# Values of the later batches in halves of 32 queries by 64 keys, a tile of their own for the gates' fifth part, and another order of layer two's mixes

## The chip, the cores and the metric

The kernel runs on one core of one Trainium2 chip. The metric is the device time in microseconds of one execution, the median of three runs. The engines of the core are TensorE (PE; its weight loads are listed as PEld), VectorE (DVE), ScalarE (ACT), GpSimd (POOL), and SyncE (SP), which issues most transfers.

## The reference

Three steps stand one behind the other. `q`, `k` and `v` have 4 batches, 8 heads, 576 positions and 64 columns a head; the two layers have 512 columns outside and 2048 inside, for 4 x 576 = 2304 tokens.

```python
scores = scale * np.matmul(q, k.transpose(0, 1, 3, 2))
mask_plain = (rel >= 0) & (rel < 32)                          # heads 0 to 3
mask_dil = (rel >= 0) & (rel < 32 * 4) & (rel % 4 == 0)       # heads 4 to 7
attn = softmax(np.where(mask, scores, -1e9))
x = np.matmul(attn, v)             # heads side by side: 2304 x 512
h = x @ w_in1;  g = h - np.tanh(h);             x = g @ w_out1
h = x @ w_in2;  g = h * (1 / (1 + np.exp(-h))); out = g @ w_out2
```

A query sees 32 keys: its own and the 31 before it, in the dilated heads every fourth. With the positions of the dilated heads sorted by their remainder by 4, both kinds are a band of 32.

## The kernel before

**Attention.** The work goes by pairs: a pair is two heads (j = 0, 1) of one batch, 16 pairs in all, four for each batch. The 576 queries of a pair are cut into NB = 9 blocks of QB = 64; a block needs the KB = 96 keys from 32 before its first query to its last. The first batch (`first`) is worked in units of three blocks, with masks added in TensorE and the probabilities transposed by TensorE. From the second batch on, `transpose` turns q and k on VectorE, `products` makes scores in four tiles of TensorE at a time (two heads on separate rows, two groups of 32 queries on separate columns, each against its own 64 keys), `masks` adds the mask `near` on VectorE, and `maxima`, `exps` (ACT), `norm` follow. `p_quarter` transposes the probabilities, 32 by 32, into `pT`, which has keys on its partitions: four calls for each head, with the two corners that no query sees left at zero. `values` then makes, for each block and head, one matmul: `v` (96 keys by 64 columns) is stationary, `pT` (96 keys by 64 queries) moves, and the two heads go to separate columns of the array. The outputs are evicted twice: `x_hi` copies to the rounded part of X on ACT, `x_lo` takes the rest on VectorE. `GROUPS` splits the blocks of a pair into 5 and 4, one PSUM bank each (tiles `s` and `o`). X is a ring of two batches; columns whose place is still in use go to `late` first.

**Order.** Everything up to the first block of tokens of layer one, with the first two batches of attention, is put in order by `play`, a list scheduler that knows a cost in us for each step on each engine (`op({"T": 1.45}, ...)`) and takes what can begin first, then by rank. The later batches are put by hand into numbered ticks between the matmuls of layer one (`plan`): at a pair's tick `score`, the values of the pair before it (`other`) come first, into a bank of `ps_h` (blocks 0 to 7) and the free end of bank `o` (block 8), then the scores; then the next v is loaded.

**Layer one** goes by blocks of 512 tokens: 16 times 12 matmuls for h and 12 for y (three for each product, since weights and activations are split into a leading and a trailing part). Meanwhile the weights of layer two are prepared and stored.

**Layer two** works on 768 tokens at a time (three `Group`s) and makes each 2 by 2 product with seven instead of eight. `mixes` makes the sums and differences of x that it needs, as steps: `whole` adds the two parts of a quarter of x, `minus` takes a difference, `lead` copies the rounded part (ACT), `trail` takes the rest (VectorE). A group has eight quads (`quad`): `products`, `sums`, `gates`, which fill `G[:, quad, 0:4]`. The second product of the first group has sixteen steps f; in step f the split of the gates for step f + 2 (`parted`: ACT's copy to `gs`, VectorE's difference) comes first, then what `IN_TWO` has for f, then a load of the next group's x (f = 3 to 6) or two steps of its `mixes` (f = 7 on). In the quads of the first group `IN_ONE` puts steps that prepare `w_out2`: `out_bits`, `out_plain`, `out_mixed`. The raw words of half of these lie in `G[..., 4, :]`, the fifth part of the gates' tile, which the first group does not need; the later groups keep a sum of gates there (`combine`).

Of the kernel before, what the change touches and what calls it, by code (L numbers as in the profile page):

```python
# [35 lines left out]
def tile_kernel(  # L36
# [198 lines left out]
    GROUPS = ((0, (NB + 1) // 2), ((NB + 1) // 2, NB))  # L235

    NM = NB + GROUPS[0][1]
# [18 lines left out]
    near = cpool.tile([P, NM, NARROW], BF16, name="near")  # L256
    pT = cpool.tile([KB, NB, 2, QB], F32, name="pT")
    nc.gpsimd.memset(pT, 0.0)

    class Pair:  # L260
# [49 lines left out]
        def v_tile(self):  # L310
            if self.first and not self.dil:
                self.v = [opool.tile([KB, NB, D], F32, tag="wout", name="v") for _ in range(2)]
            else:
                if self.first and self.c == NPAIR - 1:
                    vt = g_tile([KB, 2, NB, D], F32, "v")
                else:
                    vt = inpool.tile([KB, 2, NB, D], F32, tag="v", name="v")
# [5 lines left out]
        def v_loads(self):  # L323
# [15 lines left out]
            for j in range(2):  # L339
                src = v[b, h0 + j]  # L340
                s0 = src[QB - HALO:]
                out.append(lambda e, j=j, src=src: e.dma_start(out=self.v[j][HALO:, 0, :], in_=src[0:QB]))
                out.append(lambda e, j=j, s0=s0: e.dma_start(
                    out=self.v[j][:, 1:, :],
                    in_=bass.AP(s0.tensor, s0.offset, [[D, KB], [QB * D, NB - 1], [1, D]])))
            return out

# [158 lines left out]
        def values(self, n0, n1, bank):  # L506
# [7 lines left out]
            if self.dil:  # L514
                parts = [(a, b, src[:, a - s0:b - s0]) for a, b in self.cut(s0, s1)]
            else:
                i0, i1 = s0 // DIL, s1 // DIL
                src = src.rearrange("p (i r) -> p i r", r=DIL)

                m = DIL - (self.b > 0)  # L520
                last = CLS * (DIL - 1)
                parts = [] if m == DIL else [(a, b, src[:, a - last - i0:b - last - i0, DIL - 1]) for a, b in self.cut(last + i0, last + i1)]
            out = [(self.columns(a, b), x) for a, b, x in parts]
            if not self.dil:
                a = self.column(0)
# [1067 lines left out]
```

## Time and profile before

| | |
|---|---|
| three runs | 844.59, 847.73, 846.69 us; median 846.69 |
| profiled execution | 845.14 us, its span from the first to the last instruction 843.4 us |
| TensorE busy | 828.2 us, 98% of the span, 6103 matmul records |
| VectorE, ACT, POOL busy | 68%, 50%, 24% |
| granted TensorE clock | 1.00 |
| moved by DMA | 184.58 MB, 219 GB/s in the mean |

One execution of the program is profiled. Times are us from the span's start unless marked ns. Matmuls are pipelined, so a busy TensorE is not TensorE at its peak, and the durations of records overlap; an fp32 matmul leaves two records. L408 is the line of the scores of the later batches, L510 that of the values, L578 that of all matmuls of the two layers, L748 and L749 the two steps of `parted`, L679 to L689 the steps of `mixes` (`whole`, `minus`, `lead`, `trail`).

### The profile page before, as it was taken

The page shows a single profiled execution, that of the slowest core. Times are in us where ns is not written, and L with a number is a line of the kernel's source. Part 1 is how long each engine was busy: PE and PEld are TensorE (multiplying, and loading weights), DVE is VectorE, ACT ScalarE, POOL GpSimd, SP SyncE. Part 2 cuts the span into 40 slices and gives each one's busy share as a digit, 9 for nine tenths or more (in the row PEclk, how much of TensorE's full clock was granted, in tenths as well). Part 3 has the DMA queues.
Part 4 walks back from the last instruction along what each step waited for, and adds up shares of the span by engine and source line. Part 5 has one row for each costly group of instructions (what it writes and reads, how often), then busy time and mean ns, then how long its engine had stood idle before and what let it go on. Part 6 is the DMA issues. An engine that isn't in the chain of part 4 may idle for free.

```text
span 843.4 us, 16397 instructions
## 1 busy us (share of the span) xinstructions
PE 828.2 (98%) x6103; PEld 734.7 (87%) x6103; DVE 570.5 (68%) x1010; ACT 423.6 (50%) x960; POOL 199.5 (24%) x236
## 2 busy tenths in 40 slices
PE   8899999999999999999999999999999999999998
PEld 5777778888887888888899999887999999999997
DVE  4688987466676664566665677548767888567764
ACT  5898976355555442666543343445322554233442
POOL 8555542143333331111100000001025100054000
PEclk9999999999999999999999999999999999999999
DMA  9997253655569424577679299659898677898542
GB/s 221 298 238 182 73 138 91 179 125 122 126 163 235 99 60 138 180 256 263 263 262 349 75 363 366 232 161 373 266 408 275 238 292 265 328 351 288 187 169 57
DMA packets 169856, 184.58 MB, mean 219 GB/s; under 512 B 88849, under 2 KB 132913, under 8 KB 168753
## 3 DMA queue, kind: packets, MB, share of 16 engines
q1 hardware_dynamic: 168944, 182.69, 66.9%
q8 instruction: 48, 0.79, 0.4%
q0 software_dynamic: 832, 0.85, 0.4%
q14 instruction: 32, 0.25, 0.1%
HBM read 137.89 MB, written 45.61 MB: 218 GB/s over the span
## 4 chain that ended last, share of the span: by engine, by line
PE 75%; DVE 4%; ACT 3%; DMA 1%; SPq 1%; issue 1%; POOL 1%; DVEq 0%; ACTq 0%; POOLq 0%
PE y L578 37%; PE h L578 22%; PE q L578 14%; DMA w_out<-o_mixed 1%; ACT prob L469 1%; DVE m L1215 1%; SPq L301 1%; PE h L510 1%; DVE pT L492 1%; PE s L408 0%; DVE tmp L717 0%; DVE g L605 0%; ACT gg L1451 0%; DMA o_raw<-in_moe_w_out_dram 0%; PE o L408 0%
## 5 line engine op out<-in xcount | busy, mean ns | idle before, releaser
L578 PE MATMUL y<-gg,w 128*128 128x512 f32 (+1 forms) x960 | 218.3, 370 | 2.7 <-DVE gg L1148 2.6
L578 PE MATMUL h<-x,w 128*128 128x512 f32 (+1 forms) x960 | 218.3, 370 | 0.7 <-POOL w L203 0.7
L578 PEld LDWEIGHTS y<-gg,w 128*128 128x128 f32 x960 | 167.2, 189 | 34.7 <-DVE gg L1148 3.9
L578 PEld LDWEIGHTS h<-x,w 128*128 128x128 f32 x960 | 167.3, 189 | 31.7 <-POOL w L203 1.1
L578 PE MATMUL y<-wr,gs 128*128 128x256 f32 (+1 forms) x840 | 123.5, 298 | 0.0
L578 PEld LDWEIGHTS y<-wr,gs 128*128 128x128 f32 x840 | 112.6, 191 | 4.6
L749 DVE TENSOR_TENSOR gs<-G,gs 128x768 fp32r<-128x768 f32 x72 | 70.3, 982 | 43.6 <-ACT gs L748 43.2
L748 ACT ACTIVATE gs<-G 128x768 fp32r<-128x768 f32 x72 | 60.0, 843 | 73.4 <-PE y L578 41.8
L726 ACT ACTIVATE G<-tmp 128x384 f32<-128x384 f32 (+1 forms) x48 | 33.0, 686 | 116.3 <-DVE tmp L717 116.3
L578 PE MATMUL q<-x,wr 128*128 128x384 f32 x432 | 82.7, 334 | 0.2 <-DVE tmp L717 0.2
L605 DVE TENSOR_TENSOR g<-h,g 128x512 f32<-128x512 f32 (+1 forms) x64 | 39.8, 621 | 58.8 <-ACT g L604 58.5
L763 POOL TENSOR_TENSOR G<-G 128x768 f32<-128x768 f32 (+1 forms) x24 | 42.3, 1777 | 152.1 <-DVE G L727 151.5
L578 PEld LDWEIGHTS q<-x,wr 128*128 128x128 f32 x432 | 75.5, 188 | 0.5 <-DVE tmp L717 0.5
L1451 ACT ACTIVATE gg<-g 128x512 fp32r<-128x512 f32 (+1 forms) x64 | 37.0, 579 | 75.1 <-DVE g L605 74.0
L1453 DVE TENSOR_TENSOR gg<-g,gg 128x512 fp32r<-128x512 f32 (+1 forms) x64 | 40.4, 631 | 41.7 <-ACT gg L1451 38.9
L604 ACT ACTIVATE g<-h 128x512 f32<-128x512 f32 (+1 forms) x64 | 34.6, 541 | 67.5 <-PE h L578 65.0
L727 DVE SCALAR_TENSOR_TENSOR G<-G,tmp 128x384 f32<-128x384 f32 (+1 forms) x48 | 41.4, 862 | 34.4 <-ACT G L726 34.4
L578 PE MATMUL h<-x,wr 128*128 128x384 f32 x288 | 57.8, 335 | 1.0 <-ACT tmp L721 1.0
L578 PE MATMUL y<-x,wr 128*128 128x384 f32 x288 | 57.8, 335 | 0.0
L194 POOL TENSOR_TENSOR st<-st 128x512 int32<-128x512 int32 x36 | 39.6, 1109 | 76.5 <-DVE st L190 41.7
L578 PE MATMUL q<-wr,gs 128*128 128x256 f32 (+1 forms) x348 | 57.6, 301 | 0.0
L578 PEld LDWEIGHTS h<-x,wr 128*128 128x128 f32 x288 | 50.4, 188 | 1.4 <-ACT tmp L721 1.3
(163 smaller groups left out, 1136.4 us busy)
## 6 DMA issues: line engine op xcount, KB each, us to landing
wr<-w_in SPq DMA_DIRECT2D x72, 512.0 KB
wr<-w_out SPq DMA_DIRECT2D x66, 512.0 KB
st<-in_moe_w_in_dram SPq DMA_DIRECT2D x32, 256.0 KB
st<-in_moe_w_out_dram SPq DMA_DIRECT2D x16, 512.0 KB
st_in<-in_moe_w_in_dram SPq DMA_DIRECT2D x32, 256.0 KB
w_in<-mixed SPq DMA_DIRECT2D x8, 1024.0 KB
wr<-w_in SPq DMA_DIRECT2D x24, 256.0 KB
x<-y_hi SPq DMA_DIRECT2D x6, 768.0 KB
```

The lines of the kernel that those rows point to most:

```text
L194: engine.tensor_tensor(out=high, in0=high, in1=self.low.bitcast(I32), op=ALU.add)
L301: nc.sync.dma_start(out=t[p0:p0 + 32].rearrange("r (n d) -> r n d", d=32), in_=src[b, h0 + j, :, 32 * e:32 * e + 32].rearrange("(n r) d -> ...
L578: nc.tensor.matmul(o, stat[a], mov[b], start=first and n == 0, stop=last and n == 2, skip_group_check=more)
L604: nc.scalar.activation(out=g, in_=h, func=AF.Tanh)
L605: nc.vector.tensor_tensor(out=g, in0=h, in1=g, op=ALU.subtract)
L726: nc.scalar.activation(out=g, in_=h, func=AF.Tanh, scale=0.5)
L727: return lambda: nc.vector.scalar_tensor_tensor(out=g, in0=g, scalar=1.0, in1=h, op0=ALU.add, op1=ALU.mult)
L748: nc.scalar.activation(out=gs[:, 0], in_=g, func=AF.Copy)
L749: nc.vector.tensor_tensor(out=gs[:, 1], in0=g, in1=gs[:, 0].bitcast(F32), op=ALU.subtract)
L763: (on or nc.vector).tensor_tensor(out=out, in0=x, in1=y, op=op)
L1451: nc.scalar.activation(out=gg[:, 0], in_=g, func=AF.Copy)
L1453: nc.vector.tensor_tensor(out=gg[:, 1], in0=g, in1=gg[:, 0].bitcast(F32), op=ALU.subtract)
```

## The change

From the second batch on each block's values are made in two halves: queries 0 to 31 against keys 0 to 63, and queries 32 to 63 against keys 32 to 95. The first half lies on partitions 0 to 63, the second on 64 to 127, so that v needs its rows 32 to 63 once more on partitions 96 to 127; a transfer inside SBUF puts them there, two ticks after the loads (in the second batch behind them). Each half has a bank of its own. The groups become 6 and 3 blocks, for room in bank `o`. The zeroing of `pT` goes, the mask has 13 instead of 14 blocks, and `near` is made in five copies that wait for the first pair's first unit. In layer two the fifth part of G becomes a tile `E` (before that, raw words under the same tag), `out_mixed(4)` is cut into its differences (quad 3) and its splits (quad 4), and the mixes come in another order. The cost of the second batch's values in the scheduler goes from 1.45 to 0.95, those of their evictions to 0.7 each.

```diff
-    GROUPS = ((0, (NB + 1) // 2), ((NB + 1) // 2, NB))
-    NM = NB + GROUPS[0][1]
+    GROUPS = ((0, 2 * UB), (2 * UB, NB))
+    NM = NB + 1 + UB
+    NEAR_M = NB + GROUPS[0][1]
...
-    near = cpool.tile([P, NM, NARROW], BF16, name="near")
-    pT = cpool.tile([KB, NB, 2, QB], F32, name="pT")
-    nc.gpsimd.memset(pT, 0.0)
+    near = cpool.tile([P, NEAR_M, NARROW], BF16, name="near")
+    pT1 = cpool.tile([P, NB, 2, QB], F32, name="pT")
+    pT = pT1[:KB]
+    pT2 = pT1.rearrange("p n j q -> p (n j q)")[:, :NB * QB].rearrange("p (n j q) -> p n j q", n=NB, j=2)
...
+        def double_v(self):
+            nc.sync.dma_start(out=self.vt[KB:], in_=self.vt[32:64])
...
-                other.values(0, NB - 1, ps_h.tile([P, 512], F32, tag="h", name="h"))
-                other.values(NB - 1, NB, banks[1][:, (NB - GROUPS[1][0]) * NARROW:])
+                other.halves([ps_h.tile([P, 512], F32, tag="h", name="h"), banks[1][:, (NB - GROUPS[1][0]) * NARROW:]])
...
-                for n0 in (0, NB - 1):
-                    other.x_hi(nc.scalar, n0)
-                    other.x_lo(n0)
+                for i in range(2):
+                    other.x_hi(nc.scalar, i)
+                    other.x_lo(i)
...
-            i, kk = n // 2, n // 2 + n % 2
+            i, kk = divmod(n, 2)
             p0 = QB * j + 32 * i
-            nc.vector.transpose(
-                out=pT[32 * kk:32 * kk + 32, :, j, 32 * i:32 * i + 32],
-                in_=self.p[p0:p0 + 32, :, 32 * (kk - i):32 * (kk - i) + 32],
-            )
+            k0 = KB - 32 * kk if i else 32 * kk
+            nc.vector.transpose(out=pT2[k0:k0 + 32, :, j], in_=self.p[p0:p0 + 32, :, 32 * kk:32 * kk + 32])
...
+        def halves(self, banks):
+            o = [bank[:, :NB * 32].rearrange("p (n q) -> p n q", q=32) for bank in banks]
+            for n in range(NB):
+                for i in range(2):
+                    for j in range(2):
+                        r = slice(64 * i, 64 * i + 64)
+                        nc.tensor.matmul(o[i][64 * j:64 * j + 64, n], self.v[j][r, n], pT2[r, n, j], start=True, stop=True)
...
-            return [whole(p, 4), whole(r, 3), minus(u, r, p), lead(7, u), whole(w, 1), minus(p, p, w), lead(5, p),
-                    trail(7, u), minus(r, r, p), lead(6, r), trail(5, p), whole(u, 2), minus(u, u, r), lead(4, u),
-                    trail(6, r), trail(4, u)]
+            return [whole(p, 4), whole(r, 3), minus(u, r, p), whole(w, 1), lead(7, u), minus(p, p, w), trail(7, u),
+                    lead(5, p), minus(r, r, p), trail(5, p), lead(6, r), whole(u, 2), minus(u, u, r), trail(6, r),
+                    lead(4, u), trail(4, u)]
...
-            a, b, c, d, e = (G[:, q:q + count, k] for k in range(5))
+            a, b, c, d = (G[:, q:q + count, k] for k in range(4))
+            e = E[:, q:q + count]
...
+    DOUBLE = 2
...
+        at(s0 + score + DOUBLE, p.double_v)
...
-        narrows = [op({"V": 0.35, "P": 0.9}, lambda e, g=g: narrow(e, g), [], NEXT0 - 12, port=True) for g in range(4)]
+        narrows = [op({"V": 0.35, "P": 0.9}, lambda e, g=g: narrow(e, g), x_done[0][:1], NEXT0 - 30, port=True) for g in range(4)]
+        narrows.append(op({"V": 0.15, "P": 0.3}, more, narrows, NEXT0 - 30, port=True))
...
-            return [op({"S": 0.55}, fn, [hold], r - 5 + 0.01 * n, 0.4) for n, fn in enumerate(p.v_loads())]
+            loads = [op({"S": 0.55}, fn, [hold], r - 5 + 0.01 * n, 0.4) for n, fn in enumerate(p.v_loads())]
+            return loads if p.b > 1 else [*loads, op({"S": 0.55}, lambda e, p=p: p.double_v(), loads, r - 4, 0.8)]
...
-            a = op({"T": 1.45}, lambda e, p=p: p.all_values(), [*ts, *v_in, *left["bank"]], r + 14)
+            a = op({"T": 0.95}, lambda e, p=p: p.all_values(), [*ts, *v_in, *left["bank"]], r + 14)
...
-                raw = G.bitcast(U32)[:, 4 * e:4 * e + 4, 4, :2 * P].rearrange("p k (n two) -> p k n two", two=2)
+                if e == 0:
+                    pairs_raw[q] = gates.tile([P, 2, 4, P, 2], U32, tag="E", name="raw")
+                raw = pairs_raw[q][:, e]
...
-                  3: [lambda: out_mixed(4), lambda: out_loads(6)]}
+                  3: [lambda: out_sums(4), lambda: out_loads(6)], 4: [lambda: out_split(4)]}
...
-                    G = gates.tile([P, NF // 2, 5, HALF], F32, name="G")
+                    G = gates.tile([P, NF // 2, 4, HALF], F32, name="G")
...
+                E = gates.tile([P, NF // 2, HALF], F32, tag="E", name="E")
```

In `halves`, behind the matmuls, the two banks' evictions are set up as in `values`, cut at the same columns of X and `late`, with runs of 32 queries (plain heads: 8 by 4) instead of whole blocks.

## Rows read from the trace of the kernel before

**Rows 1.** The page's busy time, share and instructions of the engines.

```profile
PE 828.2 (98%) x6103; PEld 734.7 (87%) x6103; DVE 570.5 (68%) x1010; ACT 423.6 (50%) x960; POOL 199.5 (24%) x236
```

**Rows 2.** Waits of TensorE over the span: total us, times, longest.

```profile
PE y L578 <- DVE gg L1148: 2.6, 3, 1.7
...
PE h L578 <- ACT tmp L721: 1.0, 1, 1.0
...
PE y L578 <- ACT gs L748: 0.4, 1, 0.4
```

**Rows 3.** Timeline of TensorE, 181 to 186.5: start, us, what, count.

```profile
182.25 1.15 PE L510 MATMUL h<-pT,v 96*64 96x64 f32 x32
183.23 0.29 PE L510 MATMUL o<-pT,v 96*64 96x64 f32 x4
183.45 0.76 PE L408 MATMUL s<-kT,qT 64*32 64x64 f32 x40
...
184.59 2.11 PE L578 MATMUL h<-x,w 128*128 128x512 f32 x8
```

**Rows 4.** Lines L510 and L408: ns min/median/max, first and last start.

```profile
L510 PEld LDWEIGHTS h<-pT,v x224: 132/138/139, 182.2 to 306.0; 96*64 96x64 f32 x112
L510 PE MATMUL h<-pT,v x224: 221/222/270, 182.2 to 306.1; 96*64 96x64 f32 x112
...
L408 PEld LDWEIGHTS s<-kT,qT x480: 102/107/108, 47.4 to 306.9; 64*32 64x32 f32 x160
```

**Rows 5.** Groups by form, whole span: busy us, mean ns, idle before.

```profile
L372 PE MATMUL h<-late,qin 96*64 96x96 f32 x48 | 2.9, 255 | 1.0 <-ACT kT L146 1.0
```

**Rows 6.** Timeline of SP's queue, 199 to 218.

```profile
202.44 7.46 SPq L335 DMA_DIRECT2D v<-in_v_dram  x13
```

**Rows 7.** Timeline of VectorE, 0 to 24.

```profile
7.97 0.96 DVE L148 COPY near<-mask 32x896 bf16<-32x896 bf16 x2 [6.52 <-POOL mask L224]
```

**Rows 8.** The chain that ended last, in order of time, around the fourth quad.

```profile
490.78 2.08 PE q L578 x12
...
514.33 2.08 PE q L578 x12
521.61 2.08 PE q L578 x12
```

**Rows 9.** Timeline of all engines, 494 to 516.

```profile
507.70 1.30 ACT L1376 ACTIVATE m<-m 128x512 fp32r<-128x512 f32 x2 [1.82 <-DVE m L1215]
507.92 0.41 DVE L1215 TENSOR_TENSOR m<-raw,m 128x256 f32<-128x256 f32 x1
...
508.91 0.47 ACT L721 ACTIVATE tmp<-h 128x384 f32<-128x384 f32 x1
...
509.43 1.32 PE L578 MATMUL h<-x,wr 128*128 128x384 f32 x6 [0.97 <-ACT tmp L721]
```

**Rows 10.** The same chain, in the second product of the first group.

```profile
565.77 1.36 PE q L578 x6
...
569.85 1.36 PE q L578 x6
...
587.50 1.38 PE q L578 x6
```

**Rows 11.** Timeline of all engines, 570 to 590.

```profile
576.55 0.95 DVE L683 TENSOR_TENSOR tmp<-tmp 128x768 f32<-128x768 f32 x1
...
579.15 0.96 DVE L749 TENSOR_TENSOR gs<-G,gs 128x768 fp32r<-128x768 f32 x1 [1.65 <-ACT gs L748]
579.21 2.92 PE L578 MATMUL y<-room,gs 128*128 128x512 f32 x12
...
581.83 0.94 DVE L679 TENSOR_TENSOR tmp<-x 128x768 f32<-128x768 f32 x1
...
583.71 0.84 ACT L748 ACTIVATE gs<-G 128x768 fp32r<-128x768 f32 x1 [2.31 <-POOL G L194]
```

**Rows 12.** Timeline of SP's queue, 579.5 to 581.

```profile
580.10 0.33 SPq L1199 DMA_DIRECT2D wr<-w_in  x1
```

More of the change, by code (lines that the diff above doesn't have):

```diff
@@ L316, in v_tile @@
                 else:
-                    vt = inpool.tile([KB, 2, NB, D], F32, tag="v", name="v")
+                    vt = inpool.tile([KB if self.first else P, 2, NB, D], F32, tag="v", name="v")
                 self.vt = vt
@@ L514, in values @@
             if self.dil:
-                parts = [(a, b, src[:, a - s0:b - s0]) for a, b in self.cut(s0, s1)]
+                out = [([X[:, w, self.c, self.column(s0):self.column(s0) + s1 - s0] for w in range(2)], src)]
             else:
[L517 to L522, printed above, removed]
@@ L523, in values @@
-            out = [(self.columns(a, b), x) for a, b, x in parts]
-            if not self.dil:
                 a = self.column(0)
-                x = X[:, :, self.c, a:a + CLS * m].rearrange("p w (r i) -> p w i r", i=CLS)[:, :, i0:i1]
-                out.append(([x[:, w] for w in range(2)], src[:, :, :m]))
+                x = X[:, :, self.c, a:a + S].rearrange("p w (r i) -> p w i r", i=CLS)[:, :, s0 // DIL:s1 // DIL]
+                out = [([x[:, w] for w in range(2)], src.rearrange("p (i r) -> p i r", r=DIL))]
@@ L528, in values @@
             self.left[n0] = out
+        def halves(self, banks):
[5 more added lines that the diff above has]
+                        nc.tensor.matmul(o[i][64 * j:64 * j + 64, n], self.v[j][r, n], pT2[r, n, j], start=True, stop=True)
+            for i in range(2):
+                if self.dil:
+                    out = [([d.rearrange("p (n i q) -> p n i q", i=2, q=32)[:, :, i] for d in self.columns(a, b)],
+                            o[i][:, a // QB:b // QB]) for a, b in self.cut(0, S)]
+                else:
+                    e = 32 // DIL
+                    src = o[i].rearrange("p n (e r) -> p n e r", r=DIL)
+                    last, a, m = CLS * (DIL - 1), self.column(0), DIL - 1
+                    x = X[:, :, self.c, a:a + CLS * m].rearrange("p w (r n i e) -> p w n i e r", r=m, i=2, e=e)[:, :, :, i]
+                    out = [([d.rearrange("p (n i e) -> p n i e", i=2, e=e)[:, :, i] for d in self.columns(a, b)],
+                            src[:, (a - last) // (2 * e):(b - last) // (2 * e), :, DIL - 1]) for a, b in self.cut(last, S)]
+                    out.append(([x[:, w] for w in range(2)], src[:, :, :, :m]))
+                self.left[i] = out
@@ L563, in all_values @@
         def all_values(self):
-            for n0, n1 in GROUPS:
-                self.values(n0, n1, self.bank(n0))
+            self.halves([self.bank(i) for i in range(2)])
         def outputs(self):
             self.all_values()
-            for n0, _ in GROUPS:
-                self.x_hi(nc.scalar, n0)
-                self.x_lo(n0)
+            for i in range(2):
+                self.x_hi(nc.scalar, i)
+                self.x_lo(i)
     def passes(o, stat, mov, first, last, more=False):
@@ L1083, in narrow, with more @@
         def narrow(e, g):
-            copy(e, near[32 * g:32 * g + 32], mask[32 * g:32 * g + 32, :, 32 * (g % 2):32 * (g % 2) + NARROW])
-        narrows = [op({"V": 0.35, "P": 0.9}, lambda e, g=g: narrow(e, g), [], NEXT0 - 12, port=True) for g in range(4)]
+            copy(e, near[32 * g:32 * g + 32, :NM], mask[32 * g:32 * g + 32, :, 32 * (g % 2):32 * (g % 2) + NARROW])
+        def more(e):
+            copy(e, near[:, NM:], near[:, NM - (NEAR_M - NM):NM])
+        narrows = [op({"V": 0.35, "P": 0.9}, lambda e, g=g: narrow(e, g), x_done[0][:1], NEXT0 - 30, port=True) for g in range(4)]
+        narrows.append(op({"V": 0.15, "P": 0.3}, more, narrows, NEXT0 - 30, port=True))
         def front(p):
@@ L1118, in back @@
             ring_p.leave(*ts)
[L1119 removed]
+            a = op({"T": 0.95}, lambda e, p=p: p.all_values(), [*ts, *v_in, *left["bank"]], r + 14)
             left["pT"] = left["v"] = (a,)
             left["bank"] = ()
[L1122 to L1125 removed]
+            for i in range(2):
+                b = op({"A": 0.7}, lambda e, p=p, i=i: p.x_hi(e, i), [a], r + 15)
+                left["bank"] += (op({"V": 0.7}, lambda e, p=p, i=i: p.x_lo(i), [b], r + 15),)
         new = pairs[NPAIR:2 * NPAIR + 1]
```

27 lines of the change are left out of this document (15 added, 12 removed).

## The prediction

> **What bounds the kernel now.** I read the page first. TensorE is busy 828.2 of 843.4 us [rows 1], so the time moves only where TensorE gets less work or where a wait of TensorE comes or goes. Then the waits of TensorE over the whole span, because a filled engine leaves few of them: the largest are for gg, the second parts of layer one's gates; then one for ACT's copy into tmp and one for the split of layer two's gates, gs [rows 2]. The profiled execution took 845.14 us, 1.7 more than its span; the three runs gave 844.59, 847.73 and 846.69, so the mean of all four is 846.0, and I make the sum against that rather than against the median, 846.69. Three runs lie 3.1 us apart: a difference under about 0.5% (4.2 us) can't be told from none.
>
> Next the bursts of the values, in the timeline of TensorE. One burst of a pair is 36 records (two for each of 18 matmuls of fp32): it begins at 182.25 and the scores begin at 183.45, so it takes 1.20 us. Its first 32 records take 0.98, and of these the first pair takes longer because nothing hides its weights; the other 15 pairs come 58 ns apart. The scores after it have 72 records and take 1.14 us, up to 184.59 [rows 3]: four at a time, on separate rows and columns of the array. So four tiles do run at once, and the number of instructions is not what limits the values.
>
> **Values in halves.** The 18 matmuls of 96 keys by 64 queries become 36 of 64 keys by 32 queries, still two records each: 72 records, four to a block, one on each quarter of the array. The stationary operand is v, before and after, and it stays 64 columns wide; only the moving operand shrinks from 64 to 32 columns. So what counts is which of the two sets the 58 ns. A matmul of 96 columns takes 255 ns in the mean [rows 5] where one of 64 takes 222 [rows 4]: 32 columns are worth about 30 ns, 64 columns 55 to 60. A weight load of 64 columns takes 138 ns, one of 32 takes 107 [rows 4]. What of that keeps the tile from its matmul is seen in the first matmul of a burst, where nothing hides the load: it lasts 270 ns instead of 222, 48 more [rows 4]. So streaming 64 columns and loading 64 columns cost a tile about the same, and both fit into the 58 ns. Halve the streaming, and the loading stays. With four tiles loading at once, a block's four records still come every 55 to 58 ns, 18 of them to a burst: 1.20 us again. I take 0 for each of the 12 pairs.
>
> Both ends: if the loads did not limit, a block would come every 30 ns and a burst take 1.20 - 18 x 0.028 = 0.70 us, 12 x 0.50 = 6.0 us less. If the two halves of the rows loaded one after the other (the trace has four tiles at once only where each pair of columns has its own rows [rows 3]), a block would take 2 x 58 ns and a burst 1.04 us more, 12.5 us in all. I take the value at the nearest row, that of the burst itself, because its 48 ns of exposed load is a measurement of this very operand.
>
> Here the Trainium skill can be held against the trace. Its page "TensorEngine Tiling (Array Packing)", section "Overview", promises up to 2x for each small dimension and lets tiles load and multiply in parallel; by it the burst would halve, and the sum would be 6 us lower. Its page "TensorE: Matmul & The Clock Gate", section "LDWEIGHTS (loading the stationary operand)", says that a load costs its columns and not its rows, divided by 1.2 GHz, some 53 ns for 64 columns by estimate; by that rule the burst keeps its length. The 48 ns of the trace side with the second.
>
> **Evacuation and v's second copy.** The eviction of a pair goes from 512 + 64 columns, or 448 + 64 + 64, to two halves of 288, each cut at the same places: one to three short instructions more on ACT and as many on VectorE, off TensorE's path as long as gates come in time. Nothing waited there before, so 0; with the cover gone, a few tenths per pair at most. Groups of 6 and 3 blocks replace 5 and 4: the same columns, 0. The copy of 32 rows of v into rows 96 to 127 is one more transfer on SP per pair, behind v's 13 or 4 loads; those of one pair were issued in 7.46 us from 202.44 [rows 6], and the copy comes two ticks later, where the loads have had time to land. Values read it some ticks after that: 0, and if SP had to stand still for it, the q and k loads queued behind it have a whole pair's time in hand.
>
> **The parts around the first batch.** The four copies into near stood at 7.97 us on VectorE behind 6.5 us of waiting for the mask [rows 7]; VectorE had nothing else then. Now they wait for the first pair of the first batch and fall into a busier stretch: five copies of 0.48 us or less [rows 7], some 2 us of VectorE. The filling of pT with zeros goes. The order of the second batch is sorted anew with changed costs, which no row shows. Bound from the rows: the waits of TensorE for gg there are 2.6 us in all [rows 2]; I take 0, with 1.5 us to either side.
>
> **out_mixed in two.** The chain of waits has TensorE's q groups at 490.78, 514.33 and 521.61: a quad takes 7.28 us, and the three between the first two should take 21.84 but take 23.55 [rows 8], a loss of 1.71. The timeline shows why: ACT's copies of m wait 1.82 us for VectorE's differences, run from 507.70 to 509.00, and only then, at 508.91, comes the copy that empties the bank which TensorE wants; TensorE sits 0.97 us before its next group [rows 9], and the groups behind it come late as well. With the split moved a quad later, ACT is free at that place; what stays are four differences of 0.42 on VectorE ahead of its sums. I leave 0.2 us of the loss: -1.5 us. In the next quad two copies and two differences come after the gates, the same work as out_plain does in a quad that shows no loss.
>
> **E in its own tile, and the order of the mixes.** In the second product of the first group a step takes 4.08 us (565.77 to 569.85); from 569.85 to 587.50 are 4.33 steps' worth of time for four steps, 1.33 us lost [rows 10]. ACT's split at 583.71 stood 2.31 us behind POOL's join of the raw weights, which lie in slot 4 of G, the tile the split reads [rows 11]. With E apart this wait goes: -1.3.
>
> But the new order of the mixes puts whole(w, 1) one step earlier, right behind the difference at 576.55, which ends at 577.5 [rows 11]. It reads the half of x that was loaded last, and SP's next transfer, queued behind the end of that one (it is the wait that SP has for y_lo), starts at 580.10 [rows 12], so x is there at about 580.05. VectorE will stand from 577.5 to 580.05, add 0.94 for the sum, and only then do the split that it did at 579.15 [rows 11]: done at 581.95. TensorE begins that step at 579.9 (0.68 into the group at 579.21 [rows 11]) and wants the second part 0.45 later, at 580.35. So it loses 1.6 us, and 0.1 for the refill: +1.7. The stall moves from POOL's join to a transfer, and the place ends 0.4 worse than before.
>
> Sum: 0 - 1.5 - 1.3 + 1.7 + 0 = -1.1 us. 846.0 - 1.1 = 844.9.
>
> **Rivals.** (1) The wait for x doesn't bite, because the transfer lands 2 us earlier against VectorE: for it, E's loads write longer runs; against it, nothing in the change issues it earlier. Then -2.8: 843.2. (2) The halves do overlap as the moving operand says: -6.0 more, 838.9; against it stand the 48 ns [rows 4]. The Trainium skill's "TensorEngine Tiling (Array Packing)", section "Overview", leads one to it. (3) The two row halves serialise: the group of four takes up to 116 ns, and the burst up to 2.2 us: 857.4. It is slower than before by more than can be missed once the spacing passes 84 ns ((4.2 + 1.1) us over 12 x 18 blocks is 25 ns above 58). For it: no row has two tiles on the same columns. (4) The near copies and the re-sorted second batch hold back gates of layer one, some 3 us, place 20 to 60 us: 848.
>
> **Numbers.** Chances: forecast 0.50, (1) 0.20, (2) 0.10, (3) 0.12, (4) 0.08. The forecast alone, with 1.5 us for the order and the runs' own spread, lies in 842 to 848. The range has to leave (3) out but take in (1), (4) and about half of (2): 838.5 to 850. Faster by over 0.5%, that is under 842.5: (2), near half of (1), a tenth of the forecast: 0.25. Slower: (3) and the tail of (4), 0.15. The rest 0.60.
>
> **What will show it.** Bursts of 72 records of values: 1.2 us right, 0.7 for (2), 2.2 for (3). No wait of TensorE at the fourth quad, three quads in 21.9 to 22.1. No wait of ACT's gs for POOL; a wait of VectorE's L679 for the transfer of x, and of TensorE for gs, near 580. If that wait is missing, (1). The forecast is wrong if TensorE's waits before 130 us change by more than 2 us.

## The result: 857.82 us, 1.35% slower

The changed kernel took 857.82 us in the median (855.7 to 859.68) where the kernel before, beside it, took 846.69: a ratio of 1.0135, 95% interval 1.0105 to 1.0165. The forecast was 844.9 and the range ended at 850. The profiled execution took 856.9 us with a span of 855.1, 11.7 more than the 843.4 before. The time happens to be that of rival (3), by luck: the bursts show below that its mechanism was not at work.

The page's busy time of the engines, and its line on one DMA queue:

```profile
PE 834.8 (98%) x6534; PEld 739.7 (87%) x6534; DVE 572.6 (67%) x1020; ACT 425.5 (50%) x974; POOL 199.9 (23%) x237
...
q8 instruction: 52, 0.85, 0.4%
```

TensorE has 431 more matmul records, near the 432 that twelve pairs with 36 more each make. Queue 8 carries instructions, 16 KB a packet. 13,068 records of TensorE (matmuls and weight loads) over 52 packets are 251 to a packet; with the 228 semaphore and 3 drain instructions that the trace holds for TensorE beside them they are 13,299, or 256 to a packet. That it is TensorE's queue is read from this and from where its packets stand against TensorE's stands, below.

The waits of TensorE (total us, times, longest), against [rows 2]:

```profile
PE o L413 <- issue: 4.1, 2, 2.5
PE y L592 <- DVE gg L1169: 3.0, 3, 1.6
...
PE o L530 <- DMA v<-v: 1.3, 1, 1.3
PE y L592 <- DVE gs L763: 1.2, 1, 1.2
```

The copy into tmp [rows 2] is gone as a wait. New are 4.1 us in two places inside the scores (L413) in which nothing that the profile knows held TensorE back ("issue"), 1.3 us for the second copy of v, and 1.2 us for gs. That is not 11.7 yet. Counting the layers' 4,224 matmuls (L578 before, L592 after) gives the stretch in which each microsecond went; this is when the n-th of them began:

```
 matmul   before    after   later by
      0    39.13    40.62     1.49
    360   139.98   143.94     3.96
    600   198.32   202.31     3.99
    700   226.10   235.59     9.49
    960   293.81   307.21    13.40
   2000   488.88   501.90    13.02
   2200   525.26   537.02    11.76
   4200   836.20   848.11    11.91
```

The 1.49 us ahead of matmul 0 tell little: in the runs of this document it began anywhere from 38.5 to 43.4, with the halves and without. The second batch lost 2.5 us (matmuls 0 to 360), one stretch of 33 us lost 5.5 (600 to 700), one of 72 us lost 3.9 (700 to 960; the second stand, 1.64, and the wait for the copy, 1.32, lie there). The stand at out_mixed gave 1.3 back, and the place of the E tile lost 0.15. All the large losses lie where the pairs' values and scores are.

**The bursts themselves.** TensorE's timeline at the start of a burst, against [rows 3]; and the burst's line by form (ns min/median/max), against [rows 4]:

```profile
205.12 0.25 PE L530 MATMUL h<-pT,v 64*64 64x32 f32 x2
205.13 0.25 PE L530 MATMUL o<-pT,v 64*64 64x32 f32 x2
205.20 0.23 PE L530 MATMUL h<-pT,v 64*64 64x32 f32 x2
205.21 0.23 PE L530 MATMUL o<-pT,v 64*64 64x32 f32 x2
205.26 0.23 PE L530 MATMUL h<-pT,v 64*64 64x32 f32 x2
```

```profile
L530 PEld LDWEIGHTS h<-pT,v x252: 129/135/135, 186.2 to 319.2; 64*64 64x64 f32 x126
L530 PE MATMUL h<-pT,v x252: 211/219/240, 186.2 to 319.2; 64*64 64x32 f32 x126
```

Four records come every 58 ns (205.20 to 205.26), and the scores begin at 206.30: 1.18 us where it was 1.20. The weight load takes 135 ns, as against 138 [rows 4], although the moving operand has half the columns.

**The stand behind them.** All engines at the end of this burst (start, us, engine, what; idle before it):

```profile
206.30 0.88 PE L413 MATMUL s<-kT,qT 64*32 64x64 f32 x48
206.46 4.61 SPq L337 DMA_DIRECT2D v<-in_v_dram  x7
...
207.00 0.38 PE L413 MATMUL o<-kT,qT 64*32 64x64 f32 x11
...
209.84 0.64 PE L413 MATMUL o<-kT,qT 64*32 64x64 f32 x13 [2.46 <-issue]
```

In the middle of the scores, whose operands and bank are there, TensorE stands for 2.46 us. DMA queues from 202 to 207.5, and from 207.5 to 208.5 (packets, MB, the packets' summed time as a share of 16 engines):

```profile
q1 hardware_dynamic: 2906, 1.34, 102.6%
```

```profile
q1 hardware_dynamic: 357, 0.35, 100.2%
q8 instruction: 1, 0.02, 5.5%
```

From 202 to 207.5 the engines are full and no instruction packet runs; then one does (207.55 to 208.42 by its record), and 1.4 us behind its end TensorE goes on, at 209.84. The second stand has the same form: packet 293.08 to 294.64, stand 294.35 to 295.99. The clock by stretches (us; busy us and count of PE, PEld, DVE, ACT, POOL; granted clock; DMA share; GB/s):

```profile
205.00:207.40 2.40, 2.38 (x132) 2.06 (x132) 1.70 (x4) 1.37 (x4) 0.00 (x0) 1.00 1.05 255
207.40:209.90 2.50, 0.06 (x5) 0.06 (x7) 0.57 (x3) 0.00 (x0) 1.20 (x3) 0.81 0.79 233
209.90:215.80 5.90, 5.90 (x26) 4.57 (x26) 2.21 (x6) 1.19 (x4) 3.14 (x5) 0.50 0.26 57
215.80:222.00 6.20, 6.20 (x29) 5.10 (x28) 2.41 (x5) 4.80 (x21) 0.49 (x1) 1.00 0.13 29
```

After a stand of 2.5 us the granted clock is 0.50, the level of 1.2 GHz, for all of 209.9 to 215.8, and then 1.00 again, 2.4 GHz. What that costs is read from twelve layer matmuls at either level:

```profile
202.31 2.88 PE L592 MATMUL y<-gg,w 128*128 128x512 f32 x12
...
210.41 5.49 PE L592 MATMUL h<-x,w 128*128 128x512 f32 x12
```

So the 5.9 us at half clock did about half the work, a loss of some 3 us, and 2.46 of stand and 3 of clock are the 5.5 us of that stretch.

### The profile page after: what moved, and what is told of

It is laid out like the page before. It is cut to its first block, busy times and chain, and to the rows that moved or that the text cites. A ratio compares the mean times of both kernels' runs of the same rounds, so it can differ in the third digit from the quotient of the medians.

```text
span 855.1 us, 17310 instructions
## 1 busy us (share of the span) xinstructions
PE 834.8 (98%) x6534; PEld 739.7 (87%) x6534; DVE 572.6 (67%) x1020; ACT 425.5 (50%) x974; POOL 199.9 (23%) x237
## 2 busy tenths in 40 slices
DMA packets 168900, 186.42 MB, mean 218 GB/s; under 512 B 89041, under 2 KB 131057, under 8 KB 167793
## 4 chain that ended last, share of the span: by engine, by line
PE 84%; DMA 6%; ACT 3%; SPq 2%; issue 2%; DVE 2%; POOL 1%; ACTq 0%; DVEq 0%; POOLq 0%
PE y L592 40%; PE h L592 26%; PE q L592 15%; DMA v<-in_v_dram 2%; DMA x<-y_lo 1%; DMA st<-in_moe_w_in_dram 1%; DMA v<-v 1%; SPq L337 1%; PE s L413 1%; SPq L303 1%; ACT prob L473 1%; PE h L530 1%; PE o L530 0%; ACT st L180 0%; PE o L413 0%
## 5 line engine op out<-in xcount | busy, mean ns | idle before, releaser
L592 PE MATMUL y<-gg,w 128*128 128x512 f32 (+1 forms) x960 | 219.3, 371 | 3.0 <-DVE gg L1169 3.0
L592 PE MATMUL h<-x,w 128*128 128x512 f32 (+1 forms) x960 | 221.4, 374 | 0.7 <-POOL w L203 0.7
L592 PEld LDWEIGHTS y<-gg,w 128*128 128x128 f32 x960 | 168.1, 190 | 35.2 <-DVE gg L1169 4.3
L592 PEld LDWEIGHTS h<-x,w 128*128 128x128 f32 x960 | 169.3, 191 | 33.0 <-POOL w L203 1.1
L592 PE MATMUL y<-wr,gs 128*128 128x256 f32 (+1 forms) x840 | 123.5, 298 | 0.0
L592 PEld LDWEIGHTS y<-wr,gs 128*128 128x128 f32 x840 | 112.6, 191 | 4.6
L763 DVE TENSOR_TENSOR gs<-G,gs 128x768 fp32r<-128x768 f32 x64 | 63.6, 999 | 40.4 <-ACT gs L762 40.0
L762 ACT ACTIVATE gs<-G 128x768 fp32r<-128x768 f32 x64 | 53.5, 844 | 69.2 <-PE y L592 44.5
L592 PE MATMUL q<-x,wr 128*128 128x384 f32 x432 | 82.8, 335 | 0.0
L592 PEld LDWEIGHTS q<-x,wr 128*128 128x128 f32 x432 | 75.5, 188 | 0.5 <-DVE tmp L731 0.5
L592 PE MATMUL y<-x,wr 128*128 128x384 f32 x288 | 57.7, 334 | 0.0
L592 PE MATMUL h<-x,wr 128*128 128x384 f32 x288 | 57.7, 334 | 0.0
L592 PE MATMUL q<-wr,gs 128*128 128x256 f32 (+1 forms) x348 | 57.6, 301 | 0.0
L592 PEld LDWEIGHTS q<-wr,gs 128*128 128x128 f32 x348 | 49.3, 191 | 2.3
L592 PEld LDWEIGHTS y<-x,wr 128*128 128x128 f32 x288 | 50.5, 188 | 0.2 <-DVE x L652 0.2
```

The lines of the kernel that those rows point to most:

```text
L592: nc.tensor.matmul(o, stat[a], mov[b], start=first and n == 0, stop=last and n == 2, skip_group_check=more)
L762: nc.scalar.activation(out=gs[:, 0], in_=g, func=AF.Copy)
L763: nc.vector.tensor_tensor(out=gs[:, 1], in0=g, in1=gs[:, 0].bitcast(F32), op=ALU.subtract)
```

## The experiments

### Which part, and whose instructions

First the parts apart: the halves alone (with the second copy of v, the groups of 6 and 3, the five copies into near and the planner's entries), and everything but them, with the new and with the old order of the mixes.

```
halves_alone:   G of five slots, out_mixed in one, mixes in the old order
rest_alone:     values(0, NB - 1) and values(NB - 1, NB) as before
tile_and_split: as rest_alone, and mixes in the old order
```

> The kernel before with the halves, the second copy of v and the planner's entries for them, but with its own gates' tile, mixes and order of mixes. Theory A (the stretch from 36 to 300 us, where the changed kernel lost 13.4 us by its layer matmuls, is the halves' doing: more instructions than TensorE has at hand in one burst, a stand, and the halved clock behind it): 858 to 861 us. Rival B (the loss comes from elsewhere, the halves cost what their 58 ns cadence says): 845 to 848 us.

> The kernel before with everything but the halves: the gates' tile in two, the split of the output mix moved one tick on, the other order of layer two's mixes. Theory A: the stand at 508 us goes (1.2 to 1.5 us), at 583 us one stand of 1.3 us is exchanged for one of 1.2 us: 844.5 to 846 us. Rival B (the rest carries the loss): 855 us or more.

> As the run with everything but the halves, but with the old order of the mixes, which leaves the multiplication that waits for the transfer of x in its later place. If that wait is the whole reason why the place at 583 us gave nothing, both stands go: 842.5 to 844.5 us, 1 to 1.5 us under the run with the new order. If the gates' tile gives nothing whatever the order: as the run with the new order, 844.5 to 846 us.

Halves alone took 856.94 us (ratio 1.0147, 1.0127 to 1.0167), with the same two stands in the scores, 4.3 us. The rest alone took 844.14 (0.9993, 0.9978 to 1.0008), with the old order 844.9 (0.9996, 0.9982 to 1.0011). The loss is that of the halves and what came with them, as theory A has it, and the order of the mixes makes no difference that shows.

Then the number of instructions by itself, in the kernel before, with its values of 96 keys by 64 queries:

```
-                    for i in range(2):
+                    for i in ((0, 0, 1) if self.b > 1 else (0, 1)):      # scores_half_twice
+                    for i in ((0, 0, 1, 1) if self.b > 1 else (0, 1)):   # scores_all_twice
```

> The kernel before (values in 64 by 96) with the first 32 queries' score matmuls of every block done twice in batches three and four, with the same result: 36 more matmul records per pair, as many instructions in a burst as the halves have, at 16 ns each, 0.57 us per pair and 4.6 us in all. Theory A2: waits for issue of 1 us or more in one to three of the bursts, the clock halved behind at least one: 853 to 860 us. Rival (the form of the halves, their two row tiles or the second copy of v makes the stands, not the number): no such wait, 849 to 851.5 us.

> The same with all score matmuls done twice: 72 more matmul records per pair, 360 instructions in a burst, 9.1 us by itself. Theory A2: waits for issue in more of the bursts than with half of them, 858 to 872 us. Rival: no such wait, 853.5 to 856 us.

857.29 us (1.0132, 1.01 to 1.0165) and 877.46 (1.0385, 1.0347 to 1.0423). With half of them twice the 36 repeated records cost 28 ns each, with all the 72 cost 14, and not 16: about 1.0 us a burst in both, so the times say less than was expected of them; the waits say more. Waits of TensorE, half twice and then all twice:

```profile
PE h L578 <- issue: 1.5, 1, 1.5
```

```profile
PE o L408 <- issue: 15.5, 7, 3.2
```

And the first of the seven, in TensorE's timeline of the run with all scores twice:

```profile
185.29 0.87 PE L408 MATMUL o<-kT,qT 64*32 64x64 f32 x47
189.33 0.45 PE L408 MATMUL o<-kT,qT 64*32 64x64 f32 x17 [3.17 <-issue]
```

All seven bursts of 360 instructions stand, each until 1.2 to 1.6 us after an instruction packet has ended (the packet of this one from 186.42 to 187.84), without any halves, any second copy of v or any doubled row tile. With 288 instructions one burst of seven is followed by a stand. So more instructions in a burst make stands without the halves.

### Attempts to part the burst

Two kernels put a tick of layer matmuls between the halves and the scores; two others issue v's transfers or its second copy at another tick.

```
values_tick_earlier: at(s0 + score - 1, lambda: p.values_of(other)); load_v, double_v one tick earlier too
scores_tick_later:   STEPS = (0, 5, 6, 7, 8, 11), the halves and load_v kept at s0 + 4, double_v at s0 + 6
scores_later_copy_earlier: as scores_tick_later, DOUBLE = 1
copy_tick_earlier:   DOUBLE = 1
v_tick_later:        at(s0 + score + 1, p.load_v), DOUBLE = 3
```

> The changed kernel with each later pair's halves, the copies of x behind them, v's transfers and the second copy of v one tick (3.6 us of layer matmuls) ahead of the scores, so that 144 instructions and 144 instructions no longer make one burst of 288. Theory A2 (the burst outruns TensorE's instruction fetch): the stands of 2.46 us at 207 us and 1.64 us at 294 us go, and with the first the halved clock of 6.8 us: 848 to 851 us, no wait for issue above 0.6 us in the scores, clock 1.0 from 80 us on. Theory A1 (the fetch is late because of v's packets, however the instructions lie): waits for issue of 1 to 3 us stay, 854 to 859 us.

> The changed kernel with the halves, the copies of x, v's transfers and the second copy of v where they were, and the later pairs' scores and all that follows from them (exponentials, norm, transposes of p) one tick later: the burst of 288 instructions is parted by a tick of layer matmuls, and, other than when the halves went a tick earlier, p's transposes and v have as long as before or nearly so. Theory A2 (burst longer than what is fetched): no wait for issue above 0.6 us in the scores or behind them, 848 to 852 us. Theory A1 (v's packets hold the fetch back, whatever the burst): waits for issue of 1 us or more stay, 854 to 859 us.

> The same with the second copy of v one tick earlier. If the two losses add, the wait for the copy (1.3 us) goes too: 847 to 851 us, which would still be slower than the kernel before by the 2 to 3 us that the second batch lost. A version at or under 845 us would show that the whole loss was the bursts and the copy.

> The changed kernel with the second copy of v issued one tick earlier, one tick after v's own transfers in place of two. If the copy is only issued too late, the wait of 1.3 us at 268 us goes and nothing takes its place: 856 to 857 us. If SyncE's standing for v's transfers then holds back the q and k loads behind it: a new wait at the transposes of q and k, 858 us or more.

> The changed kernel with v's 13 transfers (and the second copy behind them) issued one tick later, so that they no longer leave while the burst of halves and scores runs. Theory A1 (TensorE's instruction fetch stands behind v's packets on the DMA engines and so comes too late): the stands of 2.46 us at 207 us and 1.64 us at 294 us and the halved clock behind the first go, 847 to 851 us. Theory A2 (the burst of 288 instructions simply outruns the fetch, whatever else is transferred): the stands stay, 856 to 860 us.

They took, in this order, 866.31 us (1.0248), 873.34 (1.032), 872.22 (1.031), 856.38 (1.0122, 1.0096 to 1.0148) and 883.24 (1.0452, 1.0436 to 1.0467). The first three miss both theories' numbers: parting the burst brought the halves to a place where p's transposes are not done, and TensorE waits there. Waits of TensorE in scores_tick_later:

```profile
PE h L529 <- issue: 6.0, 4, 2.5
PE h L529 <- DVE pT L496: 3.3, 2, 1.7
PE o L529 <- DVE pT L496: 3.1, 6, 0.6
```

The largest of these come early in the halves of five pairs, 1.6 to 2.5 us each, no instruction packet runs beside them, and where the profile names a releaser it is VectorE's transposes of p. Behind them lie 17 us at a granted clock of 0.50, in four stretches. The scores of this kernel have no wait for issue. Those of values_tick_earlier have one of 1.6 us, at 216.6 us, with a packet from 215.52 to 216.76: parted bursts of 144 can stand too, if a packet comes late enough. So the times say nothing on the fetch, and the waits only that parting the burst is no full cure. v_tick_later shows another thing, in its waits:

```profile
PE o L530 <- DMA v<-v: 22.5, 5, 8.9
```

One tick taken from v's way puts the copy on TensorE's path in five pairs. With the copy a tick earlier its wait disappears, as expected, but two others appear at the halves, of 1.1 us in the sixth burst (marked issue) and of 0.5 in the fifth (for p's transposes), and the time can't be told from the changed kernel's; the stands of 2.4 and 1.6 us in the scores remain.

### What makes the fetch late

The same burst without v's transfers, then the doubled scores without them. Both kernels leave v of the later pairs out and multiply by the v of the pair ahead:

```
-            at(s0 + score, p.load_v)
+            at(s0 + score, lambda: p.same_v(other))     # self.v = other.v
```

> The changed kernel without v's 13 transfers and the second copy of v for the later pairs, which multiply by the v of the pair ahead of them (so the output of batches three and four is left wrong). The halves, their order and their number of instructions stay. Theory A1 (v's packets hold the fetch back): the stands inside the scores at 207 and 294 us go, 847 to 851 us. Theory A2: they stay at 1.5 us or more each, 854 to 858 us, less 1.3 us for the wait for the copy, which must go in both.

> The kernel before with all score matmuls done twice, and without v's transfers for the later pairs, which multiply by the v of the pair ahead of them. With v's transfers there were seven waits for issue of 1.0 to 3.2 us, 15.5 us in all. Theory A2: seven waits of about the same length, 873 to 879 us. Theory A1: under 5 us of such waits, 860 to 867 us. Both at work: 5 to 12 us.

848.95 us (1.0048, 1.0028 to 1.0067) and 876.15 (1.036). The changed kernel loses its stands in the scores, so A2 falls as it stood: 288 instructions don't always make a stand. The doubled scores keep theirs, so A1 falls as well: v's packets are not needed. Their waits:

```profile
PE o L411 <- issue: 15.1, 6, 3.6
```

What both have in common is when the fetch comes. In after_no_v, DMA queues from 201 to 202.6:

```profile
q1 hardware_dynamic: 1269, 0.16, 61.7%
q8 instruction: 1, 0.02, 5.8%
```

This packet starts at 201.05, 0.1 us ahead of SyncE's issue of w_out<-o_plain (201.13) and of TensorE's record 3951 (201.17; matmuls and weight loads, counted from 0). The changed kernel has the same records in the same order. Its record 3951 begins at 202.53, just behind the issue of o_plain (202.46) as in the other run, but its packet starts at 207.55, 5.0 us behind that record; in between lie full DMA engines and four transfers of output weights (1.5 MB). TensorE stood after 284 more records. So here 284 records would have had to last 7.3 us (the 5.0, the packet's 0.9 and the 1.4 behind it), and a burst goes through 263 of them in 2.26 us (205.12 to 207.38). That it was the full engines which held the packet back is argued from this pair of runs.

If that is so, the stands must move when the instruction stream is shifted against the program, nothing else changed:

```
-        for n in range(WARM):
-            nc.tensor.matmul(bank, warm[:, 0:P], warm, start=True, stop=True)
...
+        for n in range(51):                                 # shift_78; shift_24: 8 of 512 columns and 16 of 128
+            nc.tensor.matmul(bank[:, 0:P], warm[:, 0:P], warm[:, 0:P], start=True, stop=True)
```

> The changed kernel with its 12 warming matmuls of 512 columns at the start cut into 51 of 128: the same columns less a little, 39 matmuls and so 78 instructions more ahead of everything, nothing else changed. In the run without v's transfers a fetch began when TensorE was at its 3951st record, 21 records ahead of the third pair's burst, and the fetches come 251 records apart on average; counted so, in the changed kernel fetches fall due 27 and 24 records ahead of the two bursts that stood, and 78 instructions put each of them over 100 records ahead, with none closer than 36 to any burst's first record. Theory A4 (a stand needs a fetch that falls due just ahead of a burst while the tick's transfers fill the DMA engines): no wait for issue above 0.6 us in any later pair's burst, 848 to 851 us. Rival (these two bursts stand for a reason of their own): 1.5 us or more at the same two bursts, 855 to 860 us.

> The same with 8 warming matmuls of 512 columns and 16 of 128: 24 instructions more. Theory A4: the fetches of the two bursts that stood now fall due 50 records ahead, 5 us before the burst, and their stands go; the fetch of the burst at 229 us falls due 15 records after its first one, so that if any burst stands it is that one: 848 to 855 us, no stand at 207 and 294 us. Rival: the stands stay at these two bursts, 855 to 860 us.

> The kernel before with the same 78 instructions more at the start. Its bursts have 216 instructions, and about 285 are at hand when a fetch falls due (in the changed kernel TensorE stood 284 records after the place at which the run without v's transfers fetched). Theory A4: no burst can outrun the fetch wherever it falls due, no wait for issue above 0.6 us, 843.5 to 847 us. Rival (the kernel before was only lucky in its place): waits of 1 us or more, 848 us or more.

853.95 us (1.0093, 1.0058 to 1.0129), 855.47 (1.0128, 1.0085 to 1.0172) and 847.78 (1.002, 1.0005 to 1.0035). TensorE's timeline in shift_78, its second stand among the waits, and the waits in shift_24:

```profile
226.91 0.33 PE L413 MATMUL o<-kT,qT 64*32 64x64 f32 x9
230.04 0.42 PE L413 MATMUL o<-kT,qT 64*32 64x64 f32 x15 [2.81 <-issue]
```

```profile
PE s L413 <- issue: 1.3, 1, 1.3
```

```profile
PE o L413 <- issue: 1.7, 1, 1.7
PE y L592 <- issue: 1.7, 2, 0.8
```

With 78 instructions more, the stands of the second and the sixth burst (207 and 294 us in the changed kernel) are gone, and the third and the seventh, which had none, stand for 2.81 and 1.28 us. With 24 more, the second burst's is gone, the sixth's stays (1.74 us), and two of 0.8 us appear behind the third and the seventh. So the place in the stream decides which burst stands, and the rival falls. My count of where it would decide was wrong: the third and the seventh burst of shift_78 should have been safe, and the sixth and the seventh of shift_24 too.

The traces show why. I had counted 251 records to a packet; counted are all of TensorE's instructions, 256 to a packet. Number them from 0 and the packets of queue 8 from 1: in all twenty runs the j-th packet belongs to instruction 193 + 256j, its border. In 1,001 such pairs the instruction never begins sooner than 1.2 us after its packet's end, and at each of the 32 stands of 0.8 us and more in the later pairs that have a packet beside them it begins 1.2 to 1.6 us after. The changed kernel stands at 4289 and 6081 (j = 16 and 23). At bursts of 288 instructions TensorE stood only where a border fell 236 to 315 instructions behind the burst's first, and there in 18 of 30 cases: at 263 and 287 in the changed kernel, at 261 and 236 in shift_78. The other waits for issue of that size lie off the borders and are not the fetch's.

The seventh burst of shift_78 also corrects the account of full engines. Its packet runs from 316.40 to 317.33, ahead of v's first issue at 316.69, and this is the stretch before it:

```profile
314.00:316.40 2.40, 2.40 (x79) 1.89 (x77) 1.37 (x3) 0.63 (x1) 0.20 (x1) 1.00 0.00 0
```

The DMA engines' share is 0.00 for 2.4 us, and the stand comes all the same. So full engines are not a condition of a stand; what made this packet late is open.

The kernel before keeps its scores free of it: its largest wait for issue is the 0.5 us it had unshifted. Its 0.2% are not a stand of that kind; its profiled execution has 3.4 us at a granted clock of 0.50 in the second batch, from 72.1 us on.

Last, the output weights moved, to see whose packets hold the fetch:

```
-        OUT_STEPS = (2, 5, 8, 11, 14, 17, 20, 24)
+        OUT_STEPS = (3, 6, 9, 12, 15, 18, 21, 25)
...
-        OUT_MIXED = (5, 8, 11, 14, 17, 20, 24, 28)
+        OUT_MIXED = (6, 9, 12, 15, 18, 21, 25, 28)
```

> The changed kernel with the preparation of layer two's output weights (its loads, stores and mixes) one tick later from the third batch on, so that its 1.5 MB per three ticks no longer leave in the tick of the burst; v's transfers stay there. If the weights' packets hold the fetch back: no stand of 1.5 us or more at 207 and 294 us, 848 to 853 us. If v's packets do: both stay, 856 to 860 us. If the place in the stream alone decides, whatever is transferred: both stay as well, with the fetch again some 5 us after TensorE's 3951st record.

> The kernel before with the same move of the output weights. It has no stand to lose: 844 to 848 us, unless the weights come too late for layer two, which would show as a wait there.

853.41 us (1.0085, 1.0052 to 1.0118) and 845.27 (0.9992, 0.9974 to 1.0009). The edit did less than it says: near the second burst only o_mixed went behind v's transfers; o_plain (issued at 198.89) and two loads of o_raw stayed ahead of the burst. Both stands stayed, 3.8 us in all:

```profile
PE o L413 <- issue: 3.8, 2, 2.6
```

Record 3951 came at 198.97, just behind o_plain's issue again, and the packet at 203.97, again 5.0 us later. v's first packet was issued at 202.89, 3.9 us after that record: v's own packets can't be most of this delay. Which of the others are was not isolated.

### The second batch

```
+            if self.b == 1: (transposes of p, values, copies of x, planner's costs as in the kernel before; no second copy of v)
```

> The changed kernel with the second batch's values as in the kernel before (64 by 96, its transposes of p, its copies of x, no second copy of v, its costs in the planner). If the planned second batch loses its 2 to 3 us by the halves, the 360th matmul of the layers comes at 140 to 142 us in place of 143.9; if by the gates of near or the noise of the start, at 143 us or later. The time says little: 288 instructions less ahead of the later pairs move every fetch, by theory A4 to within 15 records of three bursts, so that stands remain: 852 to 860 us.

854.29 us (1.0095, 1.0063 to 1.0128). The 360th matmul began at 140.29: the batch took 100.0 us from its first layer matmul, where it took 100.9 before, 103.3 in the changed kernel and 104.4 in halves_alone; rest_alone had 98.7, tile_and_split 101.4. These are single executions. Over all kernels here, the eleven with halves in the second batch took 100.5 to 107.0 us, 103.3 in the mean, the nine without 98.7 to 102.0, 100.4 in the mean. So the 2.5 us came with the halves there too, though no single run shows it. Stands stayed, as expected of the theory, one of 3.9 us behind the second burst and one of 1.3 us in the fifth:

```profile
PE h L628 <- issue: 3.9, 1, 3.9
```

## Why the prediction was wrong

**The values' term, 0, was wrong in what it left out.** Its cadence was right: 58 ns for four records and 1.18 us for a burst, so rivals (2) and (3) are both refuted. That the weight load of 64 columns sets the 58 ns is argued and not shown: the scores, whose load has 32 columns and takes 107 ns [rows 4], have four records every 56 ns as well, and a fixed time for each record on its tile would give the same. (The prediction's columns were also read low: 255 less 222 is 33 ns for 32 columns and so 66 for 64, not 55 to 60; and a burst halved is 7.2 us less over twelve pairs, not 6. Nothing hung on either.) The rule of the Trainium skill that a load costs its columns and not its rows ("TensorE: Matmul & The Clock Gate", "LDWEIGHTS (loading the stationary operand)") agrees with the trace, 135 ns for 64 rows and 138 for 96; the 2x of "TensorEngine Tiling (Array Packing)", "Overview", did not appear (that tiles load and multiply in parallel stands on that page under "Key Properties"). What failed is the sentence "the number of instructions is not what limits the values". It was read from a burst of 216 instructions that ran without a gap, and carried over to one of 288. In the changed kernel two bursts of seven outran the instruction fetch: 4.1 us of stands, and some 3 us of clock at 1.2 GHz behind the first. The trace of before had the queue's packets; I didn't hold them against the bursts.

The Trainium skill has a page on it, "Runtime: NRT & Kernel Launch", section "Instruction fetch mechanics": instructions come in blocks of 16 KiB, 256 instructions each, over a DMA queue that the engine's sequencer drives, and crossing a block's border is mostly hidden. The 256 instructions to a packet agree; that the crossing is hidden holds in the kernel before and fails here, by 2.46 and 1.64 us at two borders.

**v's second copy, 0.** The copy was not early enough in every pair. In the fifth burst SyncE issues it behind the stores of y, at 261.79, and TensorE waits 1.3 us for it; with v a tick later it waits 22.5 us in five pairs. The loads and the copy, which must wait for them to land, follow one another in one pair's time.

**The second batch, 0 with 1.5 us to either side.** It lost 2.5 us, with the halves. This is the place of rival (4), and not its cause: the gates' wait for gg grew by 0.4 us alone. What of the 2.5 us is the wait of 0.9 us marked issue in the batch's halves (at 124.4, off the borders of the fetch), the 3.4 us at half clock from 72.4 us on, or the planner's order was not parted.

**out_mixed in two, -1.5.** Right in kind and nearly in size: no stand at the fourth quad, 1.26 us less between matmuls 2000 and 2200 in the changed kernel and 1.27 in rest_alone.

**The E tile and the order of the mixes, -1.3 + 1.7.** The sum was near (+0.4 forecast, +0.15 measured), and the forecast waits are there. VectorE's timeline in the changed kernel, then TensorE's:

```profile
591.56 0.96 DVE L693 TENSOR_TENSOR tmp<-x 128x768 f32<-128x768 f32 x1 [2.29 <-DMA x<-y_lo]
592.43 0.95 DVE L763 TENSOR_TENSOR gs<-G,gs 128x768 fp32r<-128x768 f32 x1
```

```profile
593.44 1.89 PE L592 MATMUL y<-room,gs 128*128 128x512 f32 x7 [1.18 <-DVE gs L763]
```

whole(w, 1) waits 2.29 us for x (forecast 2.55), and TensorE loses 1.18 (forecast 1.6 and 0.1). But the -1.3 is a mistake that the +1.7 hid: with the old order the wait for x is gone and the place is no better. VectorE, and then TensorE, in tile_and_split:

```profile
581.82 1.68 DVE L683 TENSOR_TENSOR tmp<-tmp 128x768 f32<-128x768 f32 x1
583.42 0.95 DVE L749 TENSOR_TENSOR gs<-G,gs 128x768 fp32r<-128x768 f32 x1
```

```profile
584.42 1.90 PE L578 MATMUL y<-room,gs 128*128 128x512 f32 x7 [0.87 <-DVE gs L749]
```

ACT no longer stands for POOL, and VectorE's split is the next late thing: it stands behind a difference of x that takes 1.68 us where the one at 575.47 takes 0.95, ends at 584.37, and TensorE goes on at 584.42. The place gained 0.1 us (matmuls 2400 to 2520). The slow difference was in the trace of before:

```profile
582.81 1.68 DVE L683 TENSOR_TENSOR tmp<-tmp 128x768 f32<-128x768 f32 x1
```

I had named what was late and not what is late next.

**What stays open.** What makes a packet late, full engines or not; what sets the 58 ns; and the make-up of the second batch's 2.5 us. No kernel that was run beat both: the rest alone, at 0.9993 (0.9978 to 1.0008), can't be told from the kernel before.

## What to carry to other kernels

Count the instructions of a burst, beside the time of its tiles: in these runs no packet from 40 us on started with more than 300 of TensorE's instructions left before the one that it brings, the burst of 216 never stood, in either place of the stream that was tried, and the one of 288 did where a packet's border fell late in the burst or just behind it and the packet came late. A TensorE wait marked "issue" in the middle of work whose operands are there should be held against the packets of the instruction queue, and then against a kernel whose stream is shifted by a few dozen instructions at the start; a stand that moves belongs to the fetch, and a change that adds instructions anywhere ahead can bring it. With the stationary operand as wide as before, a narrower moving operand saved nothing here.

## What the hardware showed unasked

At the stands the instruction packet itself takes 0.9 to 1.7 us, and TensorE goes on 1.2 to 1.6 us after its end. Whether a stand in the scores was followed by a granted clock of 0.50, for 3.4 or 6.8 us, is not told by its length alone. The four of 2.2 us and more in scores_all_twice all were, and the three of 1.0 to 1.7 us there were not; but one of 2.90 us in scores_twice_no_v (to 265.47) and one of 2.44 in copy_tick_earlier were not, and one of 1.63 in copy_tick_earlier and one of 1.74 in shift_24 were. The late fetch of the second burst in the changed kernel was so paid more than twice.
